# Second layer's third row chunk in 256-column block products, placed between the output products of chunks 0 and 1

## Chip, cores and metric

The kernel runs on one core of one Trainium2 chip. The metric is the device time of one execution in microseconds, the median over repeated executions.

## What is computed

The reference takes a windowed attention, a feed-forward layer with a squared ReLU, and a gated second layer. The change lies in the second layer alone:

```python
def _moe2_ref(x, w_gate, w_val, w_out, rms_g):      # x: 1536 x 512, w_gate, w_val: 512 x 1536
    rms = np.sqrt(np.mean(x * x, axis=-1, keepdims=True) + 1e-06)
    xn = x / rms * rms_g
    g = xn @ w_gate
    silu = g * (1.0 / (1.0 + np.exp(-g)))
    val = xn @ w_val
    return (silu * val @ w_out).astype(np.float32)   # w_out: 1536 x 512
```

## The kernel before

The 1536 rows (tokens) are three **chunks** `c` of 512, each of four groups `m` of 128 (group number g = 4c + m). The 1536 inner columns are twelve blocks `f` of 128, worked in six **rounds** `r` of two blocks (`ROUNDS2`). Every fp32 operand is split in a high and a low part, and a product is three matmuls (high by high, high by low, low by high) for each 128 of the contracted length. Each matmul has its own 128x128 weight load.

The weights come as 64-bit floats. `Units` takes them through four steps, one unit (one block of `wg`, `wv` or `wp`) at a time: a load of 512 KB into a slot of `wpool` (SyncE's queue, tiles `raw_`), two ScalarE steps (`conv_a`, tiles `x_` and `u_`), four VectorE steps (`conv_b`), and `split` (ScalarE writes the high part of a tile `w_`, VectorE the low part). The pool of the tiles `x_` (tag `x32`) has three buffers. After a `wv`, `combine` makes four 128x256 sums and differences of `wg` and `wv` (`cs`) and splits them into `cm`. `cap`, `hold` and `ahead` say how many units may be loaded, and how far the loads run ahead of the conversions.

Chunks 0 and 1 go through `pair(r, fill)`: their gate and value products are formed together by a seven-product scheme on half contractions. `six` is one such product: six matmuls of 512 columns into a PSUM bank, which is read out by ScalarE or VectorE between products that add to the same bank (`qa`, `qb`, `qc` are the banks' names). Chunk 2 goes through `plain(f)`: a gate product (bank `g2_`, 12 matmuls of 512 columns), Silu on ScalarE, a value product (`v2_`, 12 matmuls), a multiplication on VectorE. `hsplit` splits each result for the output product, `zpart(r, c, f)` (12 matmuls into four banks `z`). In rounds 1 to 4 the order on TensorE is: `pair` with the output products of the last round's chunk 2 as filling in two places, `zpart(r, 0, f)` and `plain(f)` for both blocks, `zpart(r, 1, f)` for both. In round 0 `plain` follows all output products of chunks 0 and 1; in round 5 it does too, and chunk 2's output products follow it.

The rows of chunk 2 are normalized (`norm`) and transposed on TensorE (`turn`, banks `xps`) inside round 0, two groups behind `zpart(0, 0, f)` of each block; `split_xs` splits them into `x22`.

The order on each engine is made by a scheduler when the kernel is built; `inline()` ties matmuls to the order in which the code is written.

Of the kernel before, what the change touches and what calls it, by code (L numbers as in the profile page):

```python
# [32 lines left out]
def tile_window_attention_moe_moe2(  # L33
# [198 lines left out]
    def combine(g, v_, f):  # L232
        n = DM // 2
        s = side["cb"].tile([P, 4, n], F32, tag="cs", name=f"cs{f}")
        for j, a_, b_, op in (
            (0, v_[:, 0:n], v_[:, n:], ALU.add),
            (1, s[:, 0], g[:, 0:n], ALU.subtract),
            (2, g[:, 0:n], v_[:, 0:n], ALU.subtract),
            (3, g[:, n:], s[:, 1], ALU.subtract),
        ):  # L240
# [777 lines left out]
    units1.hold, units1.ahead = 1, 4  # L1018

    def pair(r, fill):  # L1020
        fs = (FIRST2[r], FIRST2[r] + 1)
# [53 lines left out]
    def plain(f):  # L1075
        psg = bank("h", f"g2_{f}")
        with inline():
            product(psg, W[("wg", f)], xs[(2, 2)], 0, MT)
        t = t2(f"sg{f}")
        nc.scalar.activation(t, psg, AF.Silu)  # L1080
        psv = bank("a", f"v2_{f}")
        with inline():
            product(psv, W[("wv", f)], xs[(2, 2)], 0, MT)
        nc.vector.tensor_tensor(t, psv, t, op=ALU.mult)
        hq[(2, f)] = hsplit(t, CH, f"z2_{f}")
        units1.used += 2
        units1.tick()

    NR = len(ROUNDS2)
    for r in range(NR):  # L1090
# [9 lines left out]
        if r == 0:  # L1100
            for c in range(2):
                for f in fs:
                    zpart(r, c, f)
                    if norms:
                        rot["tags"] = "h" if f == fs[0] else "a"
                        for _ in range(2):
                            norm(norms.pop(0))
                            turn()
            for f in fs:
                plain(f)  # L1110
        elif r < NR - 1:
            for f in fs:
                zpart(r, 0, f)
                plain(f)
            for f in fs:
# [1 line left out]
        else:
            for c in range(2):
                for f in fs:
                    zpart(r, c, f)  # L1120
            for f in fs:
                plain(f)
# [37 lines left out]
```

## Time and profile before

| | us |
|---|---|
| median of 3 runs | 640.14 (639.49 to 640.38) |
| the profiled execution | 640.56 |
| its span, first to last instruction | 638.9 |
| TensorE matmul busy | 623.5 (98%) |
| TensorE weight load busy (beside the matmuls) | 516.4 (81%) |
| VectorE busy | 458.3 (72%) |
| ScalarE busy | 365.0 (57%) |

The span lies inside the profiled execution's own time, 1.66 us shorter. Matmuls overlap each other, so the time that one takes from the next is read from their starts, not from their durations. The second layer's products run from about 355.6 to 633 us, some 46 us to a round.

### The profile page before, as it was taken

What the parts mean: (1) busy time and instruction counts of PE and PEld (TensorE: products, weight loads), DVE (VectorE), ACT (ScalarE), POOL (GpSimd) and SP (SyncE); (2) the same over time, 40 slices, a digit from 0 to 9 for tenths busy, and PEclk for the clock granted to TensorE, in tenths of its full rate; (3) what the DMA queues carried; (4) which work ended last, traced back from release to release, by engine and by line L of the source; (5) the groups of instructions that cost most, each with busy time, mean ns of one, the idle gap of its engine ahead of it and who ended that gap; (6) DMA issues with size and microseconds to landing.
All of it is one profiled execution on the core that took longest, in us unless ns stands there. A gap on an engine that the chain in (4) does not pass through costs nothing.

```text
span 638.9 us, 9548 instructions
## 1 busy us (share of the span) xinstructions
PE 623.5 (98%) x3578; PEld 516.4 (81%) x3578; DVE 458.3 (72%) x831; ACT 365.0 (57%) x767; POOL 54.8 (9%) x81
## 2 busy tenths in 40 slices
PE   8988998999999999999999999999999999999997
PEld 6577887888888888888888888888888888888886
DVE  4799777959995289986486889489499399561323
ACT  5795566867673266564553767457367277353241
POOL 4012110000000000000000000003004004012040
PEclk9998998999999999999999999999999999999999
DMA  9999813615233123320020115218428329017063
GB/s 250 299 203 207 169 25 83 193 39 179 85 102 96 34 66 100 99 67 34 0 72 29 34 45 186 67 36 179 115 67 166 99 65 184 16 13 118 1 95 103
DMA packets 85870, 64.19 MB, mean 100 GB/s; under 512 B 51904, under 2 KB 75456, under 8 KB 85824
## 3 DMA queue, kind: packets, MB, share of 16 engines
q1 hardware_dynamic: 74576, 51.72, 27.5%
q0 software_dynamic: 11248, 11.87, 13.3%
q8 instruction: 28, 0.46, 0.3%
q14 instruction: 18, 0.15, 0.1%
HBM read 49.94 MB, written 13.63 MB: 100 GB/s over the span
## 4 chain that ended last, share of the span: by engine, by line
PE 88%; DVE 6%; DMA 2%; ACT 2%; SPq 1%; issue 1%
PE y L642 20%; PE h L620 19%; PE z L642 15%; PE qa L975 10%; PE v L620 5%; PE g L620 5%; PE qc L975 5%; PE qb L975 3%; DMA kr<-in_k_dram 1%; PE s L495 1%; PE pps L557 1%; PE xps L581 1%; PE xps L598 1%; DVE mx L531 1%; DMA vx<-in_v_dram 1%; DVE t L547 1%
## 5 line engine op out<-in xcount | busy, mean ns | idle before, releaser
L620 PE MATMUL h<-xhi,w_wi 128*128 128x512 f32 (+1 forms) x480 | 135.5, 355 | 4.5 <-ACT xhi L570 3.3
L642 PE MATMUL y<-w_wo,hhi 128*128 128x512 f32 x384 | 117.1, 393 | 1.1 <-ACT hhi L631 0.6
L620 PEld LDWEIGHTS h<-xhi,w_wi 128*128 128x128 f32 x480 | 87.0, 195 | 17.7 <-ACT xhi L570 4.4
L620 PE MATMUL h<-xlo,w_wi 128*128 128x512 f32 (+1 forms) x240 | 85.0, 355 | 1.6 <-DVE xlo L571 1.5
L642 PE MATMUL z<-w_wp,hhiz 128*128 128x512 f32 x288 | 85.8, 390 | 0.0
L642 PEld LDWEIGHTS y<-w_wo,hhi 128*128 128x128 f32 x384 | 71.4, 188 | 16.5 <-DVE w_wo L224 1.0
L1010 POOL DMA_DIRECT2D out_dram<-zs x40 | 35.5, 1173 | 493.1 <-ACT zs L1006 486.2
L642 PE MATMUL y<-w_wo,hlo 128*128 128x512 f32 x192 | 72.0, 391 | 0.0
L642 PEld LDWEIGHTS z<-w_wp,hhiz 128*128 128x128 f32 x288 | 53.9, 188 | 11.1
L620 PEld LDWEIGHTS h<-xlo,w_wi 128*128 128x128 f32 x240 | 46.8, 195 | 7.7 <-DVE xlo L571 2.2
L642 PE MATMUL z<-w_wp,hloz 128*128 128x512 f32 x144 | 53.0, 389 | 0.0
L801 ACT ACTIVATE r<-h 128x512 f32<-128x512 f32 x48 | 28.7, 599 | 40.1 <-PE h L620 40.1
L802 DVE TENSOR_TENSOR r<-h,r 128x512 f32<-128x512 f32 x48 | 32.8, 684 | 20.7 <-ACT r L801 20.7
L631 ACT CAST hhi<-r 128x512 fp32r<-128x512 f32 x48 | 29.9, 623 | 21.5 <-DVE r L802 21.2
L642 PEld LDWEIGHTS y<-w_wo,hlo 128*128 128x128 f32 x192 | 35.8, 188 | 7.4 <-issue 0.2
L632 DVE TENSOR_TENSOR hlo<-r,hhi 128x512 fp32r<-128x512 f32 x48 | 33.7, 702 | 10.0 <-ACT hhi L631 9.6
L620 PE MATMUL v<-x,w_wv 128*128 128x512 f32 x144 | 34.6, 389 | 0.0
L620 PE MATMUL g<-x,w_wg 128*128 128x512 f32 x144 | 34.6, 389 | 0.0
L1060 DVE TENSOR_TENSOR v<-qc,v 128x512 f32<-128x512 f32 x12 | 8.3, 691 | 36.4 <-ACT v L1059 36.4
L1006 ACT COPY zs<-z 128x512 f32<-128x512 f32 x48 | 26.8, 592 | 11.9 <-PE z L642 11.0
L642 PEld LDWEIGHTS z<-w_wp,hloz 128*128 128x128 f32 x144 | 27.0, 188 | 5.7
L620 PEld LDWEIGHTS g<-x,w_wg 128*128 128x128 f32 x144 | 27.0, 188 | 5.6
(205 smaller groups left out, 1216.1 us busy)
## 6 DMA issues: line engine op xcount, KB each, us to landing
out_dram<-zs POOLq DMA_DIRECT2D x40, 256.0 KB, 6.5
raw_wi<-in_moe_w_in_dram SPq DMA_DIRECT2D x16, 512.0 KB, 4.9
raw_wo<-in_moe_w_out_dram SPq DMA_DIRECT2D x16, 512.0 KB, 4.3
raw_wg<-in_moe_w_gate_dram SPq DMA_DIRECT2D x12, 512.0 KB, 3.6
raw_wv<-in_moe_w_val_dram SPq DMA_DIRECT2D x12, 512.0 KB, 3.5
raw_wp<-in_moe_w_out_dram SPq DMA_DIRECT2D x12, 512.0 KB, 5.4
kr<-in_k_dram SPq DMA_DIRECT2D x12, 256.0 KB, 4.2
qr<-in_q_dram SPq DMA_DIRECT2D x12, 256.0 KB, 4.9
```

The lines of the kernel that those rows point to most:

```text
L495: mark[("s", g)] = nc.tensor.matmul(sl[e][QT * u : QT * u + QT, p, :], qT[rr, p, QT * u : QT * u + QT], kT[rr, p, o : o + NK], start=g >= ...
L531: mark[("mx", g)] = nc.vector.reduce_max(mx[:, NPAIR * e : NPAIR * (e + 1)], sl[e], axis=AX.X, negate=True)
L620: pe["last"] = nc.tensor.matmul(ps, a_, b_, start=(i == 0), stop=(i == tot - 1))
L631: nc.scalar.copy(hi[:, 0:n], s[:, 0:n]),
L632: nc.vector.tensor_tensor(lo[:, 0:n], s[:, 0:n], hi[:, 0:n].bitcast(F32), op=ALU.subtract),
L642: pe["last"] = nc.tensor.matmul(y, a_[:, ms], b_, start=(first and i == 0), stop=(last and i == 2))
L801: nc.scalar.activation(t, ps, AF.Relu)
L802: nc.vector.tensor_tensor(t, ps, t, op=ALU.mult)
L975: last = nc.tensor.matmul(ps, w[a_][:, kk], x[b_][:, kk], start=start and n == 0, stop=n == 3 * K2 - 1, skip_group_check=not start,)
L1006: nc.scalar.copy(s, ys.pop(m))
L1010: nc.gpsimd.dma_start(out[g * P : (g + 1) * P, :], s, accum_op=ALU.add)
L1060: nc.vector.tensor_tensor(v1[f], C[f], v1[f], op=ALU.add)
```

## The change

Chunk 2 is no longer one piece of 512 rows: its groups m = 0, 1 (half a) and m = 2, 3 (half b) are put through the same seven-product scheme that `pair` uses for two chunks. `plain(f)` goes; `plain2(fs)` takes both blocks of a round, 14 calls of `six` with 256 columns, into banks `pa`, `pb`, `pc`. The operands that the scheme needs are made in round 0 by `turn2`: `xa` (half a), `xt`, `xu`, `xd` (differences of the halves). `xu` takes two slots of `wpool` for the rest of the kernel. The block stands between `zpart(r, 0, ...)` and `zpart(r, 1, ...)` in rounds 1 to 5, and before the second block's `zpart(0, 1, f)` in round 0. `cs` is now two tiles of the common pool in place of one tile of its own, and `cm` is split in two halves. Loads run five units ahead in place of four, conversions stay two behind the loads in place of one, and a limit on loaded units falls from 12 to 11 of the 14 slots.

```diff
     def combine(g, v_, f):
         n = DM // 2
-        s = side["cb"].tile([P, 4, n], F32, tag="cs", name=f"cs{f}")
+        s = [t2(f"cs{f}_{j}") for j in range(2)]
...
-        nc.scalar.copy(w_[:, 0], s)
-        nc.vector.tensor_tensor(w_[:, 1], s, w_[:, 0].bitcast(F32), op=ALU.subtract)
+        for j in range(2):
+            hi, lo = (w_[:, e, 2 * j : 2 * j + 2] for e in range(2))
+            sv = s[j].rearrange("p (a n) -> p a n", a=2)
+            nc.scalar.copy(hi, sv)
+            nc.vector.tensor_tensor(lo, sv, hi.bitcast(F32), op=ALU.subtract)
...
+    def turn2(ps, m):
+        n = DM // 2
+        ms = slice(m % 2 * P, m % 2 * P + P)
+        if m < 2:
+            hi_lo(q2["a"][0][:, :, ms], q2["a"][1][:, :, ms], ps, KD)
+            rows[m] = t2(f"xq{m}")
+            nc.scalar.copy(rows[m], ps)
+            return
...
+        x0 = rows.pop(m - 2)
+        ta = t2(f"tq{m}")
+        nc.vector.tensor_tensor(ta[:, 0:n], ps[:, 0:n], x0[:, 0:n], op=ALU.subtract)
+        nc.vector.tensor_tensor(ta[:, n:], ps[:, n:], ta[:, 0:n], op=ALU.subtract)
+        hi_lo(q2["t"][0][:, :, ms], q2["t"][1][:, :, ms], ta, KD)
+        nc.vector.tensor_tensor(x0[:, 0:n], ta[:, n:], x0[:, 0:n], op=ALU.subtract)
+        nc.vector.tensor_tensor(x0[:, n:], x0[:, n:], ta[:, n:], op=ALU.subtract)
+        hi_lo(q2["d"][:, 0 : KD // 2, ms], q2["d"][:, KD // 2 :, ms], ps[:, n:], KD // 2)
+        hi_lo(q2["u"][0][:, :, ms], q2["u"][1][:, :, ms], x0, KD)
...
-                units1.cap = NW - 2
+                units1.cap = NW - 3
...
-    units1.hold, units1.ahead = 1, 4
+    units1.hold, units1.ahead = 2, 5
...
-    def plain(f):
-        psg = bank("h", f"g2_{f}")
-        with inline():
-            product(psg, W[("wg", f)], xs[(2, 2)], 0, MT)
...
+    def plain2(fs):
+        wg, wv, cs = blocks(fs)
...
+        for f in fs:
+            A[f] = bank("h", f"pa{f}")[:, a]
+            six(A[f], wg[f][0], xa[0], True)
+            z[f] = t2(f"sg{f}")
+            nc.scalar.copy(z[f][:, a], A[f])
+        for f in fs:
+            C[f] = bank("a", f"pb{f}")[:, a]
+            six(C[f], wg[f][1], xa[1], True)
+            nc.vector.tensor_tensor(z[f][:, a], C[f], z[f][:, a], op=ALU.add)
+            nc.scalar.activation(z[f][:, a], z[f][:, a], AF.Silu)
+        for f in fs:
+            six(A[f], cs[f][1], xt[1], False)
+            nc.scalar.copy(z[f][:, b], A[f])
+        units1.tick()
+        for f in fs:
+            C[f] = bank("a", f"pc{f}")[:, a]
+            six(C[f], cs[f][0], xt[0], True)
+        for f in fs:
+            six(A[f], cs[f][2], xu[0], False)
+            v1[f] = t2(f"vg{f}")
+            nc.scalar.copy(v1[f][:, b], A[f])
+            nc.vector.tensor_tensor(v1[f][:, b], C[f], v1[f][:, b], op=ALU.add)
+        for f in fs:
+            six(A[f], wv[f][1], xu[1], False)
+            nc.vector.tensor_tensor(z[f][:, a], A[f], z[f][:, a], op=ALU.mult)
+        for f in fs:
+            six(C[f], cs[f][3], xd, False)
+            nc.vector.tensor_tensor(z[f][:, b], C[f], z[f][:, b], op=ALU.add)
+            nc.scalar.activation(z[f][:, b], z[f][:, b], AF.Silu)
+            nc.vector.tensor_tensor(z[f][:, b], z[f][:, b], v1[f][:, b], op=ALU.mult)
+            hq[(2, f)] = hsplit(z[f], CH, f"z2_{f}")
+        units1.used += 4
         units1.tick()
...
+        for c in range(2):
             for f in fs:
-                zpart(r, 1, f)
...
+                if (c, f) == (1, fs[1 if r == 0 else 0]):
+                    plain2(fs)
+                zpart(r, c, f)
```

The scheduler's order is shown at two places; a number that ends a name is a buffer's. The first is ScalarE in round 1, where it serves chunk 2's first block (f = 2, the tiles `sg2`, `vg2`; `x_`, `u_`, `w_` and `cm` are weight work, `zs` evicts an output product of chunk 0). Before:

```order
L1080 ACTIVATE sg2_4378<-g2_2_4365 128x512
L223 CAST w_wp4_4567<-x_wp4_4405 128x512
L243 CAST cm5_4478<-cs5_4473 128x1024
L203 ACTIVATE x_wg6_4574<-raw_wg6_4409 128x512
L203 ACTIVATE x_wv6_4633<-raw_wv6_4411 128x512
L223 CAST w_wp5_4626<-x_wp5_4485 128x512
L204 ACTIVATE u_wv6_4634<-raw_wv6_4411 128x512
L631 CAST hhiz2_2_4394<-sg2_4378 128x512
```

Now:

```order
L1121 COPY sg2_4470<-pa2_4463 128x256
L1121 COPY sg3_4479<-pa3_4472 128x256
L203 ACTIVATE x_wv5_4652<-raw_wv5_4318 128x512
L1126 ACTIVATE sg2_4470<-sg2_4470 128x256
L203 ACTIVATE x_wp4_4660<-raw_wp4_4365 128x512
L1129 COPY sg2_4470<-pa2_4463 128x256
L1126 ACTIVATE sg3_4479<-sg3_4479 128x256
L1129 COPY sg3_4479<-pa3_4472 128x256
L1137 COPY vg2_4551<-pa2_4463 128x256
L204 ACTIVATE u_wp5_4685<-raw_wp5_4606 128x512
L1137 COPY vg3_4560<-pa3_4472 128x256
L223 CAST w_wv5_4666<-x_wv5_4652 128x512
```

One Silu read the bank of a whole product; now six copies of 256 columns read banks to which TensorE goes on adding, with weight steps between them.

The second place is VectorE, where the combined weights `cm3` of round 1's second block are made. Before, it stands in round 0, among the last steps of chunks 0 and 1 (`hloz1`) and the splits of chunk 2's transposes (`x22`):

```order
L241 TENSOR_TENSOR cs3_4105<-cs3_4105,x_wg3_4029 128x256
L632 TENSOR_TENSOR hloz1_0_3848<-u0_3760,hhiz1_0_3847 128x512
L571 TENSOR_TENSOR x22_1_3707<-xps2_8_3894,x22_0_3706 128x4x128
L241 TENSOR_TENSOR cs3_4105<-x_wg3_4029,cs3_4105 128x256
L210 TENSOR_SCALAR x_wp3_4117<-x_wp3_4117 128x512
L571 TENSOR_TENSOR x22_1_3707<-xps2_9_3902,x22_0_3706 128x4x128
L632 TENSOR_TENSOR hloz1_1_3861<-u1_3768,hhiz1_1_3860 128x512
L211 TENSOR_SCALAR x_wp3_4117<-x_wp3_4117 128x512
L214 SCALAR_TENSOR_TENSOR x_wp3_4117<-raw_wp3_4033,x_wp3_4117 128x512
L244 TENSOR_TENSOR cm3_4110<-cs3_4105,cm3_4110 128x1024
```

Now it stands behind round 0's whole chunk 2, among rows that read round 1's first banks (`qb2`, `qb3`):

```order
L217 ISA x_wv3_4182<-x_wv3_4182,u_wv3_4183 128x1024
L211 TENSOR_SCALAR x_wp2_4190<-x_wp2_4190 128x512
L242 TENSOR_TENSOR cs3_0_4199<-x_wv3_4182 128x256
L242 TENSOR_TENSOR cs3_1_4200<-x_wg3_4055,x_wv3_4182 128x256
L214 SCALAR_TENSOR_TENSOR x_wp2_4190<-raw_wp2_3824,x_wp2_4190 128x512
L242 TENSOR_TENSOR cs3_0_4199<-cs3_0_4199,x_wg3_4055 128x256
L224 TENSOR_TENSOR w_wv3_4196<-x_wv3_4182,w_wv3_4196 128x512
L217 ISA x_wp2_4190<-x_wp2_4190,u_wp2_4191 128x1024
L1075 TENSOR_TENSOR s2_4225<-qb2_4236,s2_4225 128x512
L242 TENSOR_TENSOR cs3_1_4200<-x_wg3_4055,cs3_0_4199 128x256
L1075 TENSOR_TENSOR s3_4234<-qb3_4245,s3_4234 128x512
L248 TENSOR_TENSOR cm3_4205<-cs3_0_4199,cm3_4205 128x512
```

Between the last row of round 0's chunk 2 (`hloz2_1`) and this row of `cm3` there stand 21 rows: 12 of 256 columns or of the kind TENSOR_SCALAR, and 9 of 512 columns or of the kind ISA. TensorE's third matmul of round 1's second `cs[1]` product waits for that row of `cm3`. In the same order, between the first read of chunk 2's last transposes (`tq2`) and the first read of a `pb` bank (`sg0`) stand 16 rows on VectorE, `tq2` among them: 10 of 256 columns and 6 of 512.

## Rows read from the trace of the kernel before

**Rows 1.** Page, part 1: busy us (share of the span) and instructions of each engine.

```profile
PE 623.5 (98%) x3578; PEld 516.4 (81%) x3578; DVE 458.3 (72%) x831; ACT 365.0 (57%) x767; POOL 54.8 (9%) x81
```

**Rows 2.** Windows: stretch, its length, busy time of each engine, by stage.

```profile
core 0: us, PE busy (x) PEld busy (x) DVE busy (x) ACT busy (x) POOL busy (x), PEclk, DMA share, GB/s
300.00:356.00 56.00, 56.00 (x264) 46.55 (x263) 38.07 (x73) 27.89 (x57) 0.00 (x0) 1.00 0.09 29
...
355.75:398.40 42.65, 42.65 (x197) 35.47 (x197) 37.39 (x73) 30.00 (x55) 0.00 (x0) 1.00 0.30 99
...
444.60:490.90 46.30, 46.30 (x206) 38.33 (x205) 34.63 (x63) 26.68 (x48) 7.16 (x9) 1.00 0.51 112
```

**Rows 3.** The chain that ended last, round 2: start us, us, engine, tile, line.

```profile
444.62 2.72 PE qa L975 x12
...
471.81 2.72 PE g L620 x12
...
490.86 2.72 PE qa L975 x12
```

**Rows 4.** Timeline of TensorE in the first layer: start us, us, instruction and count.

```profile
149.97 0.28 PE L620 MATMUL h<-xlo,w_wi 128*128 128x256 f32 x1
150.09 0.40 PE L620 MATMUL h<-xhi,w_wi 128*128 128x256 f32 x2
150.33 0.28 PE L620 MATMUL h<-xlo,w_wi 128*128 128x256 f32 x1
150.45 0.52 PE L620 MATMUL h<-xhi,w_wi 128*128 128x256 f32 x2
```

**Rows 5.** Groups by line and shape: busy us, mean ns of one, idle before.

```profile
L716 ACT COPY bt<-xps 128x256 f32<-128x256 f32 x4 | 1.5, 371 | 8.9 <-DVE ta L711 8.9
...
L1006 ACT COPY zs<-z 128x512 f32<-128x512 f32 x28 | 15.5, 590 | 7.7 <-PE z L642 7.5
...
L203 ACT ACTIVATE x_wp<-raw_wp 128x512 f32<-128x512 f32 x6 | 4.1, 680 | 0.4 <-DVE w_wp L224 0.2
...
L204 ACT ACTIVATE u_wg<-raw_wg 128x512 int32<-128x512 uint32 x4 | 2.7, 668 | 4.1 <-DMA raw_wg<-in_moe_w_gate_dram 4.1
...
L1040 DVE TENSOR_TENSOR s<-qb,s 128x512 f32<-128x512 f32 x8 | 5.5, 690 | 8.4 <-PE qb L975 7.4 <-ACT s L1041 0.7
...
L711 DVE TENSOR_TENSOR ta<-xps,ta 128x256 f32<-128x256 f32 x4 | 1.7, 416 | 0.0
```

**Rows 6.** Timeline: a product's last matmul with the next one's first; ScalarE's read.

```profile
367.60 0.62 PE L975 MATMUL qa<-xhit,cm 128*128 128x512 f32 x2
...
368.03 0.59 ACT L1059 COPY v<-qa 128x512 f32<-128x512 f32 x1 [3.46 <-PE qa L975]
```

**Rows 7.** Timeline of VectorE in round 0.

```profile
382.75 1.22 DVE L244 TENSOR_TENSOR cm<-cs,cm 128x1024 fp32r<-128x1024 f32 x1
...
393.58 0.41 DVE L241 TENSOR_TENSOR cs<-x_wg,cs 128x256 f32<-128x256 f32 x1
393.92 0.42 DVE L210 TENSOR_SCALAR x_wg<-x_wg 128x512 f32<-128x512 f32 x1
394.25 0.68 DVE L224 TENSOR_TENSOR w_wg<-x_wg,w_wg 128x512 fp32r<-128x512 f32 x1
394.85 0.42 DVE L211 TENSOR_SCALAR x_wg<-x_wg 128x512 uint32<-128x512 uint32 x1
```

**Rows 8.** Timeline of round 0: transposes of chunk 2, the product behind, ScalarE's first read.

```profile
377.35 1.03 PE L598 MATMUL xps<-ident,yp 128*128 128x128 f32 x8
378.14 0.71 PE L642 MATMUL z<-w_wp,hhiz 128*128 128x512 f32 x2
...
380.98 1.04 PE L598 MATMUL xps<-ident,yp 128*128 128x128 f32 x8
...
377.99 0.58 ACT L570 CAST x<-xps 128x512 fp32r<-128x512 f32 x1 [0.24 <-PE xps L598]
```

**Rows 9.** DMA issues: operation, KB each, median us from issue to landing.

```profile
raw_wp<-in_moe_w_out_dram SPq DMA_DIRECT2D x12, 512.0 KB, 5.4
```

More of the change, by code (lines that the diff above doesn't have):

```diff
@@ L233, in combine @@
         n = DM // 2
-        s = side["cb"].tile([P, 4, n], F32, tag="cs", name=f"cs{f}")
[L235 to L239, printed above, removed]
+        s = [t2(f"cs{f}_{j}") for j in range(2)]
+        s0, s1, s2, s3 = (s[j // 2][:, n * (j % 2) : n * (j % 2) + n] for j in range(4))
+        for o_, a_, b_, op in (
+            (s0, v_[:, 0:n], v_[:, n:], ALU.add),
+            (s1, s0, g[:, 0:n], ALU.subtract),
+            (s2, g[:, 0:n], v_[:, 0:n], ALU.subtract),
+            (s3, g[:, n:], s1, ALU.subtract),
         ):
-            nc.vector.tensor_tensor(s[:, j], a_, b_, op=op)
+            nc.vector.tensor_tensor(o_, a_, b_, op=op)
         w_ = side["cb"].tile([P, 2, 4, n], F32R, tag="cm", name=f"cm{f}", bufs=2)
-        nc.scalar.copy(w_[:, 0], s)
-        nc.vector.tensor_tensor(w_[:, 1], s, w_[:, 0].bitcast(F32), op=ALU.subtract)
+        for j in range(2):
[3 more added lines that the diff above has]
+            nc.vector.tensor_tensor(lo, sv, hi.bitcast(F32), op=ALU.subtract)
         return w_
@@ L692, in norm @@
         turns.append((g, x))
+    q2 = {}
+    def turn2(ps, m):
[6 more added lines that the diff above has]
+            return
+        if m == 2:
+            q2["u"] = [wpool.tile([P, KD, 2 * P], F32R, tag="w", name=f"xu{e}", bufs=NW) for e in range(2)]
+            q2["d"] = side["cb"].tile([P, KD, 2 * P], F32R, tag="xd", name="xd")
+        x0 = rows.pop(m - 2)
[7 more added lines that the diff above has]
+        hi_lo(q2["u"][0][:, :, ms], q2["u"][1][:, :, ms], x0, KD)
     def turn():
@@ L698, in turn @@
             ps = xtrans(x, f"xps2_{g}")
-        if c != 1:
+        if c == 2:
+            turn2(ps, m)
+            return
+        if c == 0:
             split_xs(ps, g, 2)
-            if c == 0:
-                rows[m] = t2(f"xt{m}")
-                nc.scalar.copy(rows[m], ps)
+            rows[m] = t2(f"xt{m}")
+            nc.scalar.copy(rows[m], ps)
             return
@@ L957, in tile_window_attention_moe_moe2 @@
     b22 = [tpool.tile([P, K2, CH], F32R, tag=f"b{j}", name=f"b22_{j}") for j in range(2)]
-    xs[(2, 2)] = [tpool.tile([P, KD, CH], F32R, tag=f"x{j}", name=f"x22_{j}") for j in range(2)]
+    for nm in "at":
+        q2[nm] = [tpool.tile([P, KD, 2 * P], F32R, tag=f"{nm}{e}", name=f"x{nm}{e}") for e in range(2)]
     def latest(m):
@@ L1017, in tile_window_attention_moe_moe2, with blocks @@
     x3, x4 = [[half(t, j) for t in xs[("t", 2)]] for j in range(2)]
[L1018 to L1021 removed]
+    units1.hold, units1.ahead = 2, 5
+    def blocks(fs):
         wg, wv, cs = {}, {}, {}
@@ L1030, in pair @@
             cs[f] = [[cm[:, e, j].rearrange("p (k f) -> p k f", k=K2) for e in range(2)] for j in range(4)]
+        return wg, wv, cs
+    def pair(r, fill):
+        fs = (FIRST2[r], FIRST2[r] + 1)
+        wg, wv, cs = blocks(fs)
         A, C, z0, z1, v1 = {}, {}, {}, {}, {}
@@ L1073, in pair @@
         units1.tick()
-    def plain(f):
-        psg = bank("h", f"g2_{f}")
-        with inline():
-            product(psg, W[("wg", f)], xs[(2, 2)], 0, MT)
[L1079 to L1086, printed above, removed]
+    def plain2(fs):
+        wg, wv, cs = blocks(fs)
+        n = 2 * P
+        a, b = slice(0, n), slice(n, 2 * n)
+        xa, xt, xu = ([[half(t, j) for t in q2[nm]] for j in range(2)] for nm in "atu")
+        xd = [half(q2["d"], e) for e in range(2)]
+        A, C, z, v1 = {}, {}, {}, {}
+        for f in fs:
[30 more added lines that the diff above has]
+        units1.used += 4
         units1.tick()
@@ L1099, in tile_window_attention_moe_moe2 @@
             units1.until(("wp", f))
[L1100 to L1108, printed above, removed]
-            for f in fs:
[L1110 to L1115, printed above, removed]
-                zpart(r, 1, f)
[L1117 to L1122, printed above, removed]
+        for c in range(2):
+            for f in fs:
+                if (c, f) == (1, fs[1 if r == 0 else 0]):
+                    plain2(fs)
+                zpart(r, c, f)
+                if norms:
+                    rot["tags"] = "h" if f == fs[0] else "a"
+                    for _ in range(2):
+                        norm(norms.pop(0))
+                        turn()
+        if r == NR - 1:
             for f in fs:
```

## The prediction

> **What bounds the kernel now.** I read the page first: TensorE's matmuls are busy for 623.5 of 638.9 us, VectorE for 72% [rows 1]. The windows say where the missing time lies: in the second layer TensorE is busy for the whole of each stretch, 46.30 of 46.30 in round 2 and 42.65 of 42.65 in round 0, at the full clock (1.00, that is 2.4 GHz), while VectorE has 34.63 and 37.39 [rows 2]. The chain of waits agrees: it walks along TensorE, product behind product, 2.72 us for each twelve matmuls, and a round takes 490.86 - 444.62 = 46.24 us [rows 3]. So time here is the number of matmuls by the distance between their starts, as long as nothing makes TensorE wait. Fewer columns pay at once; a new wait costs at once.
>
> **What the products cost.** Before, chunk 2 takes 24 matmuls of 512 columns for a block, 48 in a round. At 2.72 / 12 = 0.2267 us each [rows 3] that is 10.88 us a round. Now it is 14 calls of six matmuls of 256 columns, 84 in a round, each with its own weight load. The first layer already has such matmuls in a row: 149.97, 150.09, 150.33, 150.45, four of them in 0.48 us, 0.120 each [rows 4]. 84 x 0.120 = 10.08. A round gains 0.80, six rounds 4.80 us. The gain is small because half the columns cost 53% of the distance, not 50%: of the eighth of the columns that the scheme saves (288 x 512 = 147456 against 504 x 256 = 129024), more than a third goes back.
>
> By the Trainium skill (TensorE: Matmul & The Clock Gate, section Back-to-back issue gap) the distance is the columns over 2.4 GHz plus 2.5 ns, 109 ns for 256 and 216 ns for 512; an estimate from that page would be 504 x 0.109 - 288 x 0.216, or 7.3 us gained. The trace of this kernel shows some 11 ns more at both sizes, so the rows decide.
>
> **What the evictions cost.** A bank is now read more often: six reads and four more steps for a block, where one Silu and one multiplication stood. A ScalarE copy of 256 columns out of PSUM takes 371 ns where one of 512 takes 590; a VectorE step 416 against 690 [rows 5]. Neither engine is full in rounds 1 to 5 (34.63 and 26.68 of 46.30 [rows 2]), so this is free unless TensorE waits for a bank. The tightest place is `pa`: the value product adds to the bank that ScalarE has just copied to `vg`, and only one product of the other block, 6 x 0.120 = 0.72 us, lies between. In [rows 6] the first matmul, at 367.60, is a product's last, and the next product starts 0.227 later, at 367.83; ScalarE's read starts at 368.03, 0.20 behind that. 0.20 + 0.37 = 0.57, under 0.72, so the first block's copy just fits. Between it and the second block's copy the scheduler put a conversion of 0.68 (`u_wp`, priced by [rows 5]): an instruction starts some 0.1 before the one ahead of it is over (393.92 - 393.58 = 0.34 against 0.41 [rows 7]; I take the same for ScalarE), so the second copy ends at 0.20 + 0.27 + 0.58 + 0.37 = 1.42, and TensorE wants it at 2 x 0.72 = 1.44. That is too close to call it free. I take 0.1 a round in rounds 1 to 4, 0.4 in all. Round 5 has no conversions left and round 0 has none at this place. A Silu of 256 columns has no row; it lies between 0.37 and 0.59, and TensorE does not wait for it.
>
> **What turn2 costs, round 0.** VectorE is busy for 37.39 of round 0's 42.65 us before [rows 2], and now gets the differences of the halves. Take 0 as the start of the transposes of groups m = 2, 3. They take 0.79 us (378.14 - 377.35) and their first reader starts 0.64 behind their start (377.99) [rows 8]. VectorE's dense stretches show what a row takes from the next one: 0.34 for 256 columns or a TENSOR_SCALAR (393.58 to 393.92), 0.60 for 512 columns (394.25 to 394.85) [rows 7]. The 16 rows up to the first read of `pb` are 10 x 0.34 + 6 x 0.60 = 7.00 us, so that read starts at 7.64 and ends at 8.06. TensorE does an output product of 380.98 - 378.14 = 2.84 [rows 8], then `pa`, `pb` and the first `xt` products, 36 x 0.120 = 4.32, and wants that bank at 0.79 + 2.84 + 4.32 = 7.95. I take 0.3 us of waiting. `xa`, `xt`, `xu` and `xd` themselves are done earlier in this sum.
>
> **What the weight work costs, round 1.** Three conversions (`wg2`, `wv2`, `wg3`) now stand before round 0, where VectorE has 38.07 of 56 us [rows 2]: free. But they hold all three `x32` buffers until round 0's chunk 2 is over, so `wv3` and the combined weights `cm2`, `cm3` come late. Before, `cm3` was done at 382.75 + 1.22 = 383.97 [rows 7], 14 us before round 1 began at 398.4. Now take 0 as the end of round 0's block. The last result passes a VectorE step, a Silu, a VectorE step, ScalarE's and VectorE's halves of the split: 0.20 + 0.42 + 0.37 + 0.42 + 0.59 + 0.69 = 2.7, with the hops 2.9. ScalarE must first copy four output banks of chunk 1 and only then starts `wv3`: I add 0.6 of waiting. The 12 short and 10 long rows up to `cm3` are 12 x 0.34 + 10 x 0.60 = 10.1. `cm3` is there at 13.6. TensorE gets to it behind four products (z, qa, qb and the filling z), one `cs` product and two matmuls, 56 x 0.2267 = 12.7. It waits 0.9, with the semaphore 1.0. Since VectorE then has no slack for some 10 us, I add 0.3 for what follows in that round. From round 2 on the order is further ahead: `cm5` needs only `s4`, `s5` before it and is some 3 us early by the same count.
>
> **Other edits.** `xu` takes two slots and the loads have 11 units; a load of `wp` lands in 5.4 us [rows 9] and runs five units ahead, with two between load and conversion, so ScalarE should find it landed. Earlier output stores of chunk 0 and later ones of chunk 1 stay under the products. The end is as before: chunk 2's two output products come last in both.
>
> **Sum.** Against the profiled execution, 640.56 with a span of 638.9: -4.8 + 0.4 + 0.3 + 1.0 + 0.3 = -2.8, a span near 636.1. The median of the runs is 640.14, 0.42 less than the profiled one; 640.14 - 2.8 = **637.3 us**. Lower bound on what the waits cost: nothing; upper: the rivals below.
>
> **Rivals.**
> 1. *Nothing waits* (chance 0.20). If VectorE's rows hide better than I count, all 4.8 stays: 635.3. For it: TensorE did not wait in these stretches before, though VectorE had 37.39 of 42.65 [rows 2]. Against: the two sums above come out above zero.
> 2. *VectorE's lag decides* (0.15). If its rows take their whole durations, 0.42 and 0.69, the sum of round 0 is 10 x 0.42 + 6 x 0.69 = 8.3 in place of 7.0, a wait of 1.5; that of round 1 is 11.9 in place of 10.1, a wait of 2.7; with the other 0.7 (0.4 and 0.3) that is 4.9, and the gain is gone: 640.2, no change. For it: many of these rows wait for ScalarE's half of a split; against it: rows that don't wait follow each other as in [rows 7].
> 3. *A load holds up an eviction: slower* (0.08). ScalarE works in order, and `u_wp` stands between `vg2` and `vg3`. If its load has not landed, the copy behind waits and TensorE with it. Before, such waits were 4.1 us over four rounds, on `u_wg` [rows 5], harmless since no bank was queued behind. Each microsecond of it in each of rounds 1 to 4 costs 4; the gain is gone from 0.7 us a round. With 1.5, between the 1.0 of that row and a whole landing of 5.4: 637.3 + 6 = 643.3.
> 4. *Half the columns cost half* (0.03). If the 256-column matmuls of [rows 4] are held back by something in the first layer, and the distance goes with the columns, it is 0.2267 / 2 = 0.1133: 504 x 0.1133 = 57.1 us against 288 x 0.2267 = 65.3, 8.2 gained, with the same 2.0 of waits 633.9. Against: it is the same kind of matmul, with a weight load for each. The Trainium skill's rule cited above comes close to this case.
>
> The forecast itself has 0.54, from 636.0 to 638.8. A measurement of this kernel can tell 0.2%, 1.3 us, from no change: faster takes the forecast, rivals 1 and 4 (0.77), same rival 2 (0.15), slower rival 3 (0.08). The range that leaves out no more than 2 in 10 goes from rival 1 to rival 2: 635.2 to 640.2.
>
> **What would show it.** In the new profile: 84 matmuls of 256 columns in about 10.1 us in rounds 2 to 5, 45.4 to 45.6 us for a round; a wait of TensorE (or its weight load) on VectorE's `cm` of line 248 or so in round 1, near 1 us; a small one on `sg` behind `pb` in round 0. The forecast is wrong if these products lie much more than 0.12 us apart, if waits of TensorE on `vg` return every round, or if ScalarE waits for `raw_` inside the block.

## The result, and the profile after

The changed kernel is slower. Its median is 644.87 us (643.11 to 645.88, six runs), that of the kernel before 639.86 (639.13 to 641.08, six runs); the ratio is 1.0075, with a 95% interval of 1.0057 to 1.0093. The profiled execution took 645.78 us, with a span of 644.1: 5.2 us more than before, where I had forecast 2.8 less.

The page's first part answers to [rows 1]: TensorE is busy for 1.6 us less (623.5 before), although the span is 5.2 longer. So it waits where it did not wait before.

```profile
PE 621.9 (97%) x3794; PEld 524.2 (81%) x3794; DVE 476.9 (74%) x903; ACT 379.6 (59%) x833; POOL 54.8 (9%) x81
```

All waits of TensorE after 150 us, by what it waited for (total us, times, longest). The kernel before has none there.

```profile
PE xps L602 <- ACT xt L732: 1.6, 1, 1.6
PE qa L1006 <- DVE cm L248: 0.8, 1, 0.8
PE h L624 <- DVE r L831: 0.7, 1, 0.7
PE pa L1006 <- ACT vg L1137: 0.4, 1, 0.4
```

Two of them (`cm`, `vg`) are those of the prediction. The other two, `xps` (a transpose of chunk 0's rows) and `h` (a product of the first layer), are the largest together, and they lie in the *first* layer. The windows around them, of the changed kernel (the second row answers to the first of [rows 2]: DVE 38.07 there, PEclk 1.00):

```profile
250.00:300.00 50.00, 50.00 (x223) 41.40 (x222) 26.30 (x49) 19.97 (x38) 0.00 (x0) 1.00 0.06 21
300.00:356.00 56.00, 53.67 (x245) 44.04 (x244) 46.40 (x93) 29.45 (x60) 0.00 (x0) 0.97 0.15 48
...
308.00:312.00 4.00, 2.38 (x17) 1.69 (x15) 3.26 (x6) 3.40 (x8) 0.00 (x0) 1.00 0.00 0
312.00:316.00 4.00, 3.29 (x10) 2.50 (x9) 4.00 (x9) 3.83 (x8) 0.00 (x0) 0.61 0.42 131
316.00:320.00 4.00, 4.00 (x19) 3.23 (x18) 4.00 (x10) 3.06 (x6) 0.00 (x0) 0.96 0.00 0
```

and of the kernel before, in the stretch that the prediction had not looked at:

```profile
250.00:300.00 50.00, 50.00 (x223) 41.39 (x222) 44.08 (x87) 28.41 (x51) 0.00 (x0) 1.00 0.22 73
```

VectorE does 18 us less work between 250 and 300 us (44.08 to 26.30) and 8 us more from 300 to 356; from 312 to 320 it is busy without a gap. What moved is the conversion of the second layer's first weights: in the changed kernel VectorE does no step of it between 260 and 294 us. It moved to just where the first layer's chunk 0 is normalised and transposed for the second layer.

To add up where the 5.2 us lie I took the starts of single matmuls from the timeline of TensorE: the 625th and the 649th matmul of the first layer on `w_wi` (302.91 and 315.51 before, 303.35 and 320.35 now), the first `qa` of each round, and the first addition to `zp` in the last round. The first column is how far a run is ahead or behind at 303 us. All of it stems from before 146 us, the attention stage, which every execution finishes at a slightly different time and no edit touches: the 251st of these matmuls starts at 146.01 before and at 146.44 now. The end is the rest of the span, which is given to a tenth, so it is good to 0.05 us.

| us | by 303 us | 303 to 320 us, added | round 0 | 1 | 2 | 3 | 4 | 5 | end |
|---|---|---|---|---|---|---|---|---|---|
| before | 0 | 0 | 42.63 | 46.24 | 46.24 | 46.24 | 46.24 | 49.84 | 5.89 |
| changed | +0.43 | +4.41 | 42.22 | 46.69 | 45.57 | 45.57 | 46.11 | 49.05 | 8.49 |
| difference | +0.43 | +4.41 | -0.41 | +0.45 | -0.67 | -0.67 | -0.13 | -0.79 | +2.60 |

The second layer itself gained 2.2 us. The loss is at its two ends: 4.4 us in the last quarter of the first layer, 2.6 us behind the last product.

**The first end.** VectorE's timeline of the changed kernel, with the first sum of unit 0 (`cs`), the first and the last of the small steps that prepare the norm of chunk 0 (`va`, `rinv`), and the norm itself:

```profile
294.22 0.42 DVE L242 TENSOR_TENSOR cs<-x_wv 128x256 f32<-128x256 f32 x1
295.07 0.17 DVE L683 TENSOR_SCALAR va<-ss 128x4 f32<-128x4 f32 x1 [0.43 <-ACT sq L670]
...
302.83 0.17 DVE L689 RECIPROCAL rinv<-va 128x4 f32<-128x4 f32 x1
...
303.56 2.73 DVE L693 SCALAR_TENSOR_TENSOR yp<-yp,rinv,grow 128x512 f32<-128x512 f32 x4
```

The same four in the kernel before, where the sum comes 38 us and the norm 5 us earlier:

```profile
256.28 0.42 DVE L241 TENSOR_TENSOR cs<-x_wv 128x256 f32<-128x256 f32 x1
...
295.20 0.17 DVE L679 TENSOR_SCALAR va<-ss 128x4 f32<-128x4 f32 x1 [1.33 <-ACT sq L666]
...
298.49 0.17 DVE L685 RECIPROCAL rinv<-va 128x4 f32<-128x4 f32 x1
298.70 2.74 DVE L689 SCALAR_TENSOR_TENSOR yp<-yp,rinv,grow 128x512 f32<-128x512 f32 x4
```

The norm's small steps take 3.3 us from `va` to `rinv` before (295.20 to 298.49) and 7.8 us now, because rows of the conversions stand between them. In the kernel before the sums of units 0, 1 and 2 are over by 287 us. TensorE's order is fixed, so it goes on until it needs what is late:

```profile
311.46 0.66 PE L602 MATMUL xps<-ident,yp 128*128 128x128 f32 x4 [1.62 <-ACT xt L732]
312.83 0.74 PE L624 MATMUL h<-xhi,w_wi 128*128 128x512 f32 x1 [0.71 <-DVE r L831]
...
313.80 1.05 PE L624 MATMUL h<-xhi,w_wi 128*128 128x512 f32 x2
314.65 0.63 PE L624 MATMUL h<-xlo,w_wi 128*128 128x512 f32 x1
```

It idles for 1.62 and 0.71 us, with four transposes between. The longer wait ends on ScalarE, not on VectorE: ahead of `xt`, its copy of chunk 0's transposed rows, now stand two steps of a conversion, and `r`, which the second wait needs, stands behind that copy.

```profile
308.75 1.07 ACT L574 CAST xhi<-xps 128x512 fp32r<-128x512 f32 x2 [0.59 <-PE xps L602]
309.71 0.67 ACT L203 ACTIVATE x_wp<-raw_wp 128x512 f32<-128x512 f32 x1
310.27 0.66 ACT L204 ACTIVATE u_wp<-raw_wp 128x512 int32<-128x512 uint32 x1
310.83 0.58 ACT L732 COPY xt<-xps 128x512 f32<-128x512 f32 x1
```

So the norm is late by VectorE's rows, and ScalarE's rows add to it. Behind the two waits TensorE's granted clock is at the lower level: the starts lie 0.425 us apart (313.80 to 314.65 for two), about 512 columns at 1.2 GHz, and the window from 312 to 316 us shows a mean of 0.61. The eight matmuls from 312.83 to 316.35 take 3.52 us instead of 8 x 0.2267 = 1.81. Idle 2.33, slow matmuls 1.71, and the four transposes, which take some 0.3 longer: 4.3 of the 4.41. The Trainium skill (TensorE: Matmul & The Clock Gate, section Wait — 56ns, not 53.3ns?) gives 426.7 ns for 512 columns at the lower level; the trace agrees.

**The other end.** The queues of POOL and SP and their landing times (median us, last column) in the changed kernel:

```profile
631.04 3.52 POOL L1041 DMA_DIRECT2D out_dram<-zs  x4 [12.01 <-ACT zs L1037]
...
636.33 2.51 SPq L676 DMA_DIRECT2D out_dram<-zp  x4
...
out_dram<-zp SPq DMA_DIRECT2D x4, 256.0 KB, 4.7
```

and in the kernel before:

```profile
617.63 3.52 POOL L1010 DMA_DIRECT2D out_dram<-zs  x4 [1.98 <-ACT zs L1006]
...
633.73 2.37 SPq L672 DMA_DIRECT2D out_dram<-zp  x4
...
out_dram<-zp SPq DMA_DIRECT2D x4, 256.0 KB, 2.0
```

The four accumulating stores of chunk 1 (POOL's, which add to what lies in memory) are issued from 631.04 on, 5 us before the final plain stores, where they stood 16 us before them. The final stores then need 4.7 us instead of 2.0.

### The profile page after: what moved, and what is told of

It is laid out like the page before. It is cut to its first block, busy times and chain, and to the rows that moved or that the text cites. A ratio compares the mean times of both kernels' runs of the same rounds, so it can differ in the third digit from the quotient of the medians.

```text
span 644.1 us, 10119 instructions
## 1 busy us (share of the span) xinstructions
PE 621.9 (97%) x3794; PEld 524.2 (81%) x3794; DVE 476.9 (74%) x903; ACT 379.6 (59%) x833; POOL 54.8 (9%) x81
## 4 chain that ended last, share of the span: by engine, by line
PE 84%; DVE 9%; ACT 2%; SPq 2%; issue 1%; DMA 1%; DVEq 0%
PE y L646 20%; PE h L624 19%; PE z L646 14%; PE qa L1006 9%; PE qc L1006 5%; PE pa L1006 5%; PE pc L1006 3%; PE qb L1006 2%; PE s L499 1%; SPq L362 1%; PE xps L585 1%; PE pb L1006 1%; PE pps L561 1%; DMA kr<-in_k_dram 1%; PE xps L602 1%
## 5 line engine op out<-in xcount | busy, mean ns | idle before, releaser
L646 PE MATMUL z<-w_wp,hhiz 128*128 128x512 f32 x288 | 84.1, 390 | 0.0
L646 PE MATMUL z<-w_wp,hloz 128*128 128x512 f32 x144 | 51.2, 389 | 0.0
L1037 ACT COPY zs<-z 128x512 f32<-128x512 f32 x48 | 25.5, 596 | 9.7 <-PE z L646 8.7
L564 ACT COPY pT<-pps 120x512 f32<-120x512 f32 x24 | 13.9, 613 | 15.0 <-PE pps L561 14.9
L661 DVE TENSOR_TENSOR yp<-y,yp 128x512 f32<-128x512 f32 x24 | 15.4, 682 | 8.8 <-PE y L646 8.8
L635 ACT CAST hhiz<-s 128x512 fp32r<-128x512 f32 x12 | 7.5, 622 | 24.1 <-DVE s L1100 24.1
```

What stands on the lines that cost most here:

```text
L564: mark[("pT", g)] = nc.scalar.copy(pT[:, 4 * hf : 4 * hf + 4, :], ps[0:NK].rearrange("n (h s) -> n h s", h=4))
L635: nc.scalar.copy(hi[:, 0:n], s[:, 0:n]),
L646: pe["last"] = nc.tensor.matmul(y, a_[:, ms], b_, start=(first and i == 0), stop=(last and i == 2))
L661: nc.vector.tensor_tensor(yp[g], ps, yp[g], op=ALU.add)
L1037: nc.scalar.copy(s, ys.pop(m))
```

## The experiments

Two theories for the first end. **T**: `combine`'s sums now lie in `t2`, and the buffer that they get is not free in time. **L**: the three numbers of the weight loads (cap, hold, ahead) make the conversions late. For T speaks the order in which the built program's instructions stand. In the changed kernel unit 0's first sum on VectorE waits for a semaphore of ScalarE's `sq1`, the square of chunk 0's row block 1, which last used that `t2` buffer; in the kernel before it waited only for the conversion. The program cannot place it earlier, and the conversions behind it need the `x32` buffers that it holds. VectorE's order in the kernel before:

```
L217 ISA x_wv0<-x_wv0,u_wv0 128x1024
...
L217 ISA x_wg1<-x_wg1,u_wg1 128x1024
L241 TENSOR_TENSOR cs0<-x_wv0 128x256
```

and in the changed kernel, from the same place on (the dots are 23 rows, of which none is a sum):

```
L217 ISA x_wg1<-x_wg1,u_wg1 128x1024
L224 TENSOR_TENSOR w_wv0<-x_wv0,w_wv0 128x512
...
L242 TENSOR_TENSOR cs0_0<-x_wv0 128x256
L683 TENSOR_SCALAR va0<-ss_87 128x4
```

**One part alone: combine.** The kernel before, with the new `combine`.

```diff
-        s = side["cb"].tile([P, 4, n], F32, tag="cs", name=f"cs{f}")
+        s = [t2(f"cs{f}_{j}") for j in range(2)]
...
```

> The kernel before, with one part of the change: combine writes its four sums into two buffers of the shared t2 pool (19 buffers) and not into a tile of their own. Theory T (a t2 buffer is only free once the squares of chunk 0 are done, so the conversions of the second layer's first units slide about 8 us later, onto the norm and the turn of chunk 0): the second layer's first product starts 4 to 5 us later than in the kernel before (about 360 us instead of 355.6), TensorE waits some 2 us between 309 and 313 us and its granted clock is below 1.00 for a few us after it, and the time is 643.5 to 645.5 us, ratio about 1.006 to 1.008. Rival L (the loads, held back by a cap that is one slot smaller and by other hold and ahead values, are late): no difference from the kernel before, ratio 1.000 within 0.002, first product at 355.6 us.

Measured: ratio 1.0101 (1.0084 to 1.0118), median 647.1. Between 303 and 320 us it loses 4.18 us, as the changed kernel does, with the same two waits:

```profile
PE xps L602 <- ACT xt L707: 1.6, 1, 1.6
PE qa L979 <- DVE cm L248: 1.5, 1, 1.5
PE qa L979 <- ACT s L1040: 0.8, 1, 0.8
PE h L624 <- DVE r L806: 0.7, 1, 0.7
```

The first product of the second layer stands at 358.41, not at 360, because this run was 1.36 us early by 303 us. What I had not expected are the two `qa` waits: round 1 takes 49.11 us, 2.87 more than before. The sums in `t2` hurt in the second layer as well, and that made this part alone slower than the whole change. These two waits (0.80 and 1.47 us) are together about as long as the two in the first layer, yet no lower clock follows them: the granted clock is 0.79 around the first pair and 1.00 around the second.

```profile
308.00:316.00 8.00, 5.67 (x21) 4.41 (x21) 7.93 (x18) 7.83 (x16) 0.00 (x0) 0.79 0.21 66
...
409.00:417.00 8.00, 5.72 (x24) 4.15 (x23) 8.00 (x18) 7.43 (x15) 0.00 (x0) 1.00 0.21 66
```

**The other part alone: the loads.**

```diff
-                units1.cap = NW - 2
+                units1.cap = NW - 3
...
-    units1.hold, units1.ahead = 1, 4
+    units1.hold, units1.ahead = 2, 5
```

> The kernel before with the change's three numbers of the weight loads alone: cap NW - 3 in the last chunk of the first layer, hold 2, ahead 5. Theory T: the first layer's end stays, first product of the second layer at 355.6 us within 0.5, ratio 1.000 within 0.003 (the second layer may shift by some tenths of a us, since less is loaded before it and more in it). Rival L: first product at 359 us or later, 643 us or more.

Measured: ratio 1.0014 (0.9998 to 1.0029). Nothing is added between 303 and 320 us, and all six rounds are those of the kernel before to 0.01 us; the profiled run was 1.35 us late by 303 us. L falls.

**The first end mended.** The changed kernel, with the sums of units 0 and 1 in the space that `xd` takes only later.

```diff
-        s = [t2(f"cs{f}_{j}") for j in range(2)]
+        if "d" in q2:
+            s = [t2(f"cs{f}_{j}") for j in range(2)]
+        else:
+            s = side["cb"].tile([P, 2, 2 * n], F32, tag="xd", name=f"cs{f}")
+            s = [s[:, j] for j in range(2)]
```

> The changed kernel, but the sums of units 0 and 1 (those formed in the first layer) go into a tile of their own, in the space that xd takes only in round 0, and not into t2. Theory T: the conversions stand again where they stood in the kernel before, the second layer's first product starts at 355.6 to 356.3 us, TensorE waits for nothing between 300 and 320 us with a granted clock of 1.00 there, and the time falls by 4.0 to 4.6 us against the changed kernel, to about 640.5 (ratio to the kernel before 1.001 within 0.002). Rival L: the time stays at 644.9 within 0.8.

Measured: ratio 0.9999 (0.9985 to 1.0014), median 640.9, against 1.0075. Nothing is added between 303 and 320 us. The windows there:

```profile
308.00:312.00 4.00, 4.00 (x21) 3.31 (x21) 1.82 (x3) 2.66 (x5) 0.00 (x0) 1.00 0.00 0
312.00:316.00 4.00, 4.00 (x20) 3.29 (x19) 1.78 (x4) 1.86 (x4) 0.00 (x0) 1.00 0.00 0
```

TensorE is busy throughout at a clock of 1.00, and VectorE for less than half of it. This run keeps the two halves of `cm` and the three numbers of the loads, so neither of these is the cause. T stands, from both sides. One thing is left over: this run has the changed kernel's last round, with chunk 1's four stores again 5.3 us ahead of the final ones, but there the final stores land in 3.6 us and the end takes 7.40 us, not 8.49. That late stores lengthen the end holds in both; by how much differs, from 1.5 to 2.6 us.

**The other end mended.** The changed kernel with the last round's order as before. Theory E is that the late accumulating stores make the end longer.

```diff
-                if (c, f) == (1, fs[1 if r == 0 else 0]):
+                if r < NR - 1 and (c, f) == (1, fs[1 if r == 0 else 0]):
                     plain2(fs)
...
         if r == NR - 1:
+            plain2(fs)
```

> The changed kernel, but in the last round alone the two half chunks come after both output products of chunks 0 and 1, as chunk 2's products did before. Theory E (the end of the changed kernel is longer because the four accumulating stores of chunk 1 are issued at 631 to 634.6 us and still move data when the last four stores come): those stores are issued some 10 us earlier, the last stores land in about 2 us instead of 4.7, the span from the first zp addition to its end goes from 8.5 to about 6 us, and the time falls by 2.6 us against the changed kernel, to 642.2 (ratio to the kernel before 1.0035). Rival: the tail comes from the products' order in the last two output products or from the evictions, and the time stays at 644.9 within 0.8; or TensorE waits for the last half chunks' hsplit, now directly ahead of their output products, and up to 1.5 us of the 2.6 are lost again.

Measured: ratio 1.0054 (1.0032 to 1.0076), median 643.74. Theory E and the rival's second half were both right. The end fell from 8.49 to 5.88 us, as E has it. But the half chunks' last chain (`hhiz` is its last step on ScalarE) now has no product over it:

```profile
633.47 0.73 PE L646 MATMUL z<-w_wp,hhiz 128*128 128x512 f32 x2 [1.50 <-ACT hhiz L635]
```

so the last round takes 50.89 us, 1.84 more than in the changed kernel, and only 0.8 of the 2.6 us is left. In the kernel before, the chain behind `plain`'s last product was one multiplication and the split; that of a half chunk is an addition, a Silu, a multiplication and the split.

**Both mended,** and in `plain2` the last two groups of products unit by unit.

```diff
             nc.vector.tensor_tensor(z[f][:, a], A[f], z[f][:, a], op=ALU.mult)
-        for f in fs:
             six(C[f], cs[f][3], xd, False)
```

> The changed kernel with the sums of units 0 and 1 in a tile of their own, the last round's half chunks after both output products of chunks 0 and 1, and in plain2 the last two groups of products taken unit by unit (unit f0's last product is then two products earlier, so that its chain of addition, Silu, product and split has 2.9 us and not 1.4 us before its output product). Theory: the wait of 1.5 us before the last output products is gone, the last round takes 49.0 us from its first product to the first zp addition (49.84 in the kernel before), the end after it 5.9 us as before, rounds 2 and 3 take 45.6 us, and round 1 keeps about 46.7; together 2.2 us less than before: ratio 0.9966 within 0.0015. Rival: merging the products moves the wait to the evictions of the second unit in some round, and the ratio stays at 0.999 to 1.000.

Measured: ratio 0.9978 (0.9963 to 0.9993), median 639.26. Rounds 2 and 3 take 45.45 us, round 4 45.63: the wait on `vg` is gone, since one more product now lies between the second unit's copy and its value product. The 0.18 us left in round 4 are lost at the product behind it, into `pc`. But the wait on `hhiz` only fell to 0.8 us (last round 50.17, not 49.0). My count was wrong: a unit's product is six matmuls, 0.72 us, and I had taken twelve, so the chain gained 0.7 us of cover and not 1.4. Round 1, expected to keep about 46.7 us, is at 46.98, with 1.2 us of waiting for `cm`.

**The same with hold 1 and ahead 4.**

> The same as the run with both orders mended, but with hold 1 and ahead 4, the numbers of the kernel before. Theory (the loads never bound anything here): rounds within 0.3 us of those of that run, ratio to the kernel before within 0.0015 of its ratio. Rival L2 (a load must be issued 5 units ahead because the half chunks take two more slots for xu): a wait of an ACT conversion for a load in rounds 1 to 5, and TensorE 1 us or more later in one of them.

Measured: ratio 0.998 (0.9967 to 0.9993), rounds 42.23, 47.27, 45.45, 45.45, 45.45, 50.17. TensorE waits for no load with either set of numbers. In the changed kernel ScalarE does wait longer for one than in the rows before ([rows 5], 4.1 us there), but as there TensorE waits for nothing meanwhile. The row of those steps in the changed kernel's second layer (last column: idle before, and for what):

```profile
L204 ACT ACTIVATE u_wg<-raw_wg 128x512 int32<-128x512 uint32 x8 | 5.4, 672 | 8.0 <-DMA raw_wg<-in_moe_w_gate_dram 8.0
```

**The place alone.** The kernel before, with its own 512-column products at the new place.

```diff
...
+                if r < NR - 1 and (c, f) == (1, fs[1 if r == 0 else 0]):
+                    for f_ in fs:
+                        plain(f_)
                 zpart(r, c, f)
...
```

> The kernel before with its own 512-column products of chunk 2, only put where the change puts the half chunks: both units' products between the output products of chunks 0 and 1 in rounds 0 to 4, the last round as it was. Theory (the gain of 0.8 us a round comes from the half chunks' columns and spacing, and the extra time of round 1 from cm being in use until chunk 2's products end and from the sums waiting for t2): rounds 1 to 4 take 46.24 us as before within 0.15, ratio 1.000 within 0.002. Rival (the place itself makes VectorE late in round 1): round 1 takes 46.7 us or more.

Measured: ratio 1.0023 (1.001 to 1.0036). Rounds 1 to 4 take 46.24 us each, so the place gains and costs nothing there. Missed was round 0: 44.13 us, 1.5 more, since the first product meets chunk 2's last transposes sooner than VectorE has split them:

```profile
PE g L620 <- DVE x L571: 1.0, 1, 1.0
```

**All sums in a tile of their own.** The run with both mended, but with all units' sums in one tile, and `t2` with two buffers less, so that the space is the same.

```diff
-        if "d" in q2:
-            s = [t2(f"cs{f}_{j}") for j in range(2)]
-        else:
-            s = side["cb"].tile([P, 2, 2 * n], F32, tag="xd", name=f"cs{f}")
-            s = [s[:, j] for j in range(2)]
+        s = hpool.tile([P, 2, 2 * n], F32, tag="cs", name=f"cs{f}", bufs=1)
+        s = [s[:, j] for j in range(2)]
...
-        return hpool.tile([P, DM], dt, tag="t2", name=nm, bufs=19)
+        return hpool.tile([P, DM], dt, tag="t2", name=nm, bufs=17)
```

> The run with both orders mended, but all units' sums in one tile of their own (4 KB a partition) and t2 with 17 buffers in place of 19. Theory (the cm of unit 3 is late in round 1 because its sums wait for t2 buffers as well): the wait of 0.8 us for cm in round 1 falls to 0.3 us or less, round 1 takes 45.6 to 46.2 us, ratio about 0.9956. Rival (it is late because VectorE converts four units in one clump after the half chunks of round 0, whatever the buffers): round 1 stays at 46.5 us or more and the ratio at that of the other run; or 17 buffers are too few, and the time is 1 us or more longer.

Measured: ratio 0.9953 (0.9937 to 0.9969), median 637.7. Round 1 takes 45.45 us, as rounds 2 to 4 do. The wait for `cm` is gone: VectorE ends `cm2` at 396.90, 0.4 us before round 1's start at 397.30, and `cm3` at 406.27, 9.0 us after it. The changed kernel, whose round 1 starts at 402.61, has `cm2` at 407.28, 4.7 us after that start, and `cm3` at 415.38, 12.8 after it.

```profile
395.62 1.28 DVE L249 TENSOR_TENSOR cm<-cs,cm 128x512 fp32r<-128x512 f32 x2
...
405.59 0.68 DVE L249 TENSOR_TENSOR cm<-cs,cm 128x512 fp32r<-128x512 f32 x1
```

A second measurement on another chip:

> The run with all sums in a tile of their own once more, for a comparison on the same chip: ratio 0.9953 within 0.0016, round 1 at 45.5 us, last round 50.1 us, end after the first zp addition 5.9 us.

Measured: ratio 0.9955 (0.9939 to 0.9971), median 637.89; round 1 at 45.45, last round 50.11, end 5.82. This version beats both kernels.

**Cover for the last chain.** That version with half of the last unit's output products of chunk 1 behind the half chunks.

```diff
-                zpart(r, c, f)
+                zpart(r, c, f, 0, MT // 2 if (c, f) == (1, NF2 - 1) else MT)
...
             plain2(fs)
+            zpart(r, 1, fs[1], MT // 2)
             for f in fs:
                 zpart(r, 2, f)
```

> The run with all sums in a tile of their own, and in the last round the last unit's output products of chunk 1 split by row block: those of rows 0 and 1 ahead of the half chunks, those of rows 2 and 3 (1.36 us) behind them, as cover for the last chain. Theory W (the last round of that run is 1.1 us longer than 49.0 us because the first output product of chunk 2 waits for hhiz): no wait for hhiz above 0.1 us, the last round takes 49.0 to 49.2 us and the time falls by 1.0 us, if the two stores that are now issued late (at about 626 us) land before the last four are moved, so that the end after the first zp addition stays at 5.9 us. Rival E2 (late stores of chunk 1 lengthen the end, as four of them did in the changed kernel): the last round is shorter by 1 us but the end grows to 6.5 us or more, and the time stays within 0.5 us of that run.

Measured: ratio 0.9965 (0.995 to 0.9981), median 638.62, beside 637.89 for that version on the same chip. The wait on `hhiz` is gone and the last round takes 49.65 us, 0.46 less; a wait of 0.2 us for a bank (`zs`) takes part of it. The time did not fall, for two stores of chunk 1 are now issued at 627.52:

```profile
627.52 1.75 POOL L1042 DMA_DIRECT2D out_dram<-zs  x2 [11.38 <-ACT zs L1038]
...
630.37 2.47 SPq L677 DMA_DIRECT2D out_dram<-zp  x4
...
out_dram<-zp SPq DMA_DIRECT2D x4, 256.0 KB, 3.6
```

and the end grows from 5.8 to 7.3 us. Rival E2 was right about the end, and theory E has its second proof: late accumulating stores lengthen the end. The landing times say when: in the changed kernel, in the run with the first end mended and in this one, the last accumulating store lands 7.3, 6.2 and 5.4 us after its issue, and the first final store 0.5 to 0.7 us behind that landing. So it is the last of them, and not how many there are, that the end goes by in these three runs.

All runs by the same parts; the last column but one is the profiled execution's time.

| us | by 303 us | 303 to 320 | round 0 | 1 | 2 | 3 | 4 | 5 | end | time | ratio |
|---|---|---|---|---|---|---|---|---|---|---|---|
| before | 0 | 0 | 42.63 | 46.24 | 46.24 | 46.24 | 46.24 | 49.84 | 5.89 | 640.56 | 1 |
| changed | +0.43 | +4.41 | 42.22 | 46.69 | 45.57 | 45.57 | 46.11 | 49.05 | 8.49 | 645.78 | 1.0075 |
| combine alone | -1.36 | +4.18 | 42.63 | 49.11 | 46.24 | 46.24 | 46.24 | 49.84 | 5.80 | 646.25 | 1.0101 |
| loads alone | +1.35 | 0 | 42.63 | 46.24 | 46.24 | 46.24 | 46.24 | 49.84 | 5.81 | 642.04 | 1.0014 |
| first end mended | +1.06 | 0 | 42.24 | 46.69 | 45.58 | 45.57 | 46.10 | 49.07 | 7.40 | 640.98 | 0.9999 |
| last round's order | +0.21 | +4.39 | 42.25 | 46.68 | 45.57 | 45.57 | 46.09 | 50.89 | 5.88 | 644.77 | 1.0054 |
| both, merged | -0.97 | 0 | 42.23 | 46.98 | 45.45 | 45.45 | 45.63 | 50.17 | 5.87 | 638.07 | 0.9978 |
| same, hold 1 | -0.58 | 0 | 42.23 | 47.27 | 45.45 | 45.45 | 45.45 | 50.17 | 5.87 | 638.59 | 0.998 |
| place alone | +0.96 | 0 | 44.13 | 46.24 | 46.24 | 46.24 | 46.24 | 49.84 | 5.83 | 643.02 | 1.0023 |
| sums in own tile | -0.73 | 0 | 42.45 | 45.45 | 45.45 | 45.45 | 45.45 | 50.10 | 5.88 | 636.77 | 0.9953 |
| split rows | +0.17 | 0 | 42.43 | 45.45 | 45.45 | 45.45 | 45.45 | 49.65 | 7.34 | 638.70 | 0.9965 |

## Why the prediction was wrong

The forecast was 637.3 us and faster; it came out slower. Its terms for the second layer were near. What failed were two places where I had written a cost of nothing.

**The columns** (-4.8): right. A round without waits takes 45.45 us, 0.79 less than 46.24; six of them are 4.7. In the trace of the changed kernel the last round's block takes seven times twelve matmuls from the start of the first at 616.47 to the next product's at 626.54, 10.07 us (forecast 10.08). The Trainium skill's distance (TensorE: Matmul & The Clock Gate, section Back-to-back issue gap), by which the prediction's estimate has 7.3 us gained, is given there for an isolated matmul, and the section says itself that it leaves out the weight loads. It does not hold for these matmuls, each with its own load: 0.120 us at 256 columns, not 0.109.

**`vg`** (+0.4): too small. Rounds 2 and 3 have the 0.1 of the forecast (45.57 against 45.45), but round 4 lost 0.66, so that it is some 1.0 in all, if round 1 is taken like round 2. ScalarE's timeline of the changed kernel in round 4 shows why: two conversions stand between the two copies, where I had counted one in every round.

```profile
577.04 0.37 ACT L1137 COPY vg<-pa 128x256 f32<-128x256 f32 x1 [1.79 <-PE pa L1006]
577.31 0.62 ACT L223 CAST w_wv<-x_wv 128x512 fp32r<-128x512 f32 x1
577.83 0.69 ACT L204 ACTIVATE u_wp<-raw_wp 128x512 int32<-128x512 uint32 x1
578.40 0.37 ACT L1137 COPY vg<-pa 128x256 f32<-128x256 f32 x1
```

**turn2's chain in round 0** (+0.3): right, 42.22 against 42.63 - 0.80 = 41.83, so 0.4. TensorE loses it at the predicted place, between the first `xt` products and `pc`, which needs the bank of `pb`.

**`cm3` and what follows in round 1** (+1.3): the size was right, the cause was not. Round 1 took 46.69, or 1.1 more than 45.57. I had blamed the three `x32` buffers that wait for round 0's chunk 2. The run with all sums in a tile of their own leaves that pool as it is, and the delay is gone. What held the buffers were the sums, which waited for `t2`: in the built program unit 2's first sum waits for a store of chunk 0's output to have left its buffer.

**"Three conversions (`wg2`, `wv2`, `wg3`) now stand before round 0, where VectorE has 38.07 of 56 us [rows 2]: free"**: this is the step that failed, with 4.4 us. The three are not new there: in the kernel before VectorE does them from 277.00 to 288.95 us. The step counted what is added to a long window, and not what the other edit does to the work already there: `combine`'s buffers were moved from a tile of their own into a shared pool, and that edit was priced nowhere. The first sum could no longer run ahead of chunk 0's squares, the conversions of VectorE and ScalarE slid into the one stretch where TensorE hangs on these two, and with the lower clock behind it the loss was nearly twice the wait. With the sums mended, the three conversions themselves are free: nothing is added there in the run with the first end mended, in which they still stand before round 0.

**"Earlier output stores of chunk 0 and later ones of chunk 1 stay under the products. The end is as before"**: wrong for the last round, 2.6 us in the profiled execution and 1.5 in the run with the first end mended. I looked at which product comes last, not at which store is still under way when the last stores are issued.

Rivals: the first (nothing waits) and the fourth (half the columns cost half) fell with the waits and the spacing. The second named VectorE's lag, but in rounds 0 and 1, where it cost what the forecast said. The third, the only slower one, named the loads, and the runs with the loads alone and with hold 1 clear them: `vg` in round 4 waits for conversions, not for a load. No rival had the two real causes. One piece is only argued: that the lower clock in the first layer follows from the idling before it. It came with the idling in all three profiled kernels that had it (the changed one, combine alone, last round's order); in all others the granted clock between 303 and 320 us is 1.00; no run kept TensorE busy through that wait. That idling as long as this always brings the lower clock is not so: in round 1 of combine alone it did not. What makes the difference stays open.

## What to carry to other kernels

When scratch is moved into a shared rotating pool, ask which earlier user its buffer comes from and when that one is done: the wait goes into the program's order, not only into its time, and can keep work from running ahead that no row of the profile shows as waiting. A window's mean share of an engine does not show that; look at the few microseconds where the bounding engine hangs on it, and at every engine on that path. And when the order of the last round is changed, look at the last stores and not only at the last product: four accumulating stores issued 5 us before the last stores cost 1.5 to 2.6 us here, two of them issued 3 us before 1.5, and a chain behind the last product needs something over it.

## What the runs showed of the hardware

A short idle can cost more than itself: in the changed kernel 2.33 us of waiting (1.62 and 0.71) in a stretch at full clock was followed by some 3.5 us at the lower level, and 4.4 us were lost in all. It need not: in round 1 of the run with combine alone 2.27 us of waiting (0.80 and 1.47) was followed by none.

Plain stores can be held up by accumulating ones of another queue. Four plain stores of 256 KB that land in 2.0 us by themselves took 4.7 and 3.6 us, in two runs, with four accumulating ones issued 5.3 us ahead of them, and 3.6 us with two issued 2.9 us ahead. Each time the first of them landed 0.5 to 0.7 us behind the last accumulating one.
